# First loads on two queues, rows of the mask and a scaling moved to ScalarE, and a new order for one core's attention and soft-MoE kernel

## The chip, the cores and the metric

The kernel runs on one core of a Trainium2 chip. The metric is the device time of one execution in microseconds (us). TensorE is written PE, VectorE DVE, ScalarE ACT, GpSimd POOL; SP is the engine whose queue issues nearly all DMAs. Each engine takes its own instructions in program order; semaphores make one wait for another.

## The reference

Three layers in one launch: clustered attention (a query sees only the keys whose nearest centroid is the same as its own), an MLP with the activation h cos h, and a soft mixture of experts.

```python
q_assign = np.argmax(np.einsum('bhsd,hcd->bhsc', q_n, c_n), axis=-1)
k_assign = np.argmax(np.einsum('bhsd,hcd->bhsc', k_n, c_n), axis=-1)
mask = q_assign[:, :, :, None] == k_assign[:, :, None, :]
scores = scale * np.matmul(q, k.transpose(0, 1, 3, 2))
scores = np.where(mask, scores, -1000000000.0)
scores = scores - np.max(scores, axis=-1, keepdims=True)
attn = np.exp(scores)
attn = attn / (np.sum(attn, axis=-1, keepdims=True) + 1e-09)
return np.matmul(attn, v).astype(np.float32)
...
h = x @ w_in
g = h * np.cos(h)
return (g @ w_out).astype(np.float32)
...
logits = x @ phi
```

q, k and v have 4 batches of 8 heads of 768 rows of 64, in float32; there are 16 centroids a head. The MLP goes from 512 to 2048 and back for 3072 tokens; 8 experts of 4 slots follow.

## The kernel before

**Tiling.** Two heads make a pair, and there are 16 pairs, four to a batch. A pair has 12 units: two halves of the queries (384 columns) by six tiles of 128 keys. A unit `u` of pair `i` is two scores (one a head), each a matmul on line L444 and one on L445 into a PSUM tile `s` (three buffers), an `Exp` on ACT (L448), and later the product with v, `av`, four matmuls on L457. The weights of a query are summed over the keys by POOL (`psum_add`, L472 and L475, 128x768 each), for the last half of the last pair by DVE. The maximum over the keys, which must be known before the scores, has its own 24 matmuls a pair (`smax`, L398, output `sm`), each reduced by DVE (L400).

**The mask.** It is a set of extra rows in the stacked operands `st` (three stacks, one a pair in turn): `prep_mask` makes a matrix `mt` that ACT or DVE turns into rows for q (Relu) and for k (`ksc`, `kbias`). `rows0` does it for pair 0 from PSUM, `prep_rows` for the others from a copy `z` in SBUF. The maxima go into `st` as one more row (`mrow`).

**Preparing a pair.** `load` brings q and k of a pair (four DMAs of 192 KB in 256-byte pieces), `prep_T` transposes them on PE (`tpq`, `tpk`), `prep_hi` and `prep_lo` split them in a high and a low part, `prep_cl`, `prep_ct`, `prep_mx`, `prep_eq`, `prep_eqt` and `prep_mask` find the cluster. Pair 0 is prepared before the loop, pair 1 within pair 0, every other pair two pairs ahead.

**Fill work.** Between the scores stand also the conversion of the MLP's weights (`conv_do`, steps 0 to 7, mostly DVE), a product `wphi` of one weight with phi, and `prep_vm2`, which brings the sums of v into `vm`; every fourth pair it divides four columns of `vm` by the number of keys (L386, on DVE). The last pair also prepares the first rows `x` of the MLP: `xload` (DMA), `xprep` (POOL, DVE on L108, POOL), `xprep2` (a DVE cast `xhi` on L117, then POOL `xlo` on L118). After it `hchunk(0)` begins the MLP, which wants `xhi` and `xlo`.

**What sets the order.** Tables of numbers. A number is a place in steps of a quarter unit from the start of a pair; `at4` files the function under it, and the loop over units calls what is filed. `FIRST` holds for pair 0, `POS` for the others, `NEXT` for the last but one, `LAST` for the last. PSUM tiles of these helpers come from a ring of three banks (`mbank`), so that a matmul into a bank waits until what was in it three allocations ago has been read. DMAs that depend on such work are put off by some places (`defer`, `tick`).

```python
def at4(g, q, f, *args):
    x = int(q // 1)
    at(g + x // 4, x % 4, f, *args, rank=q - x if q != x else 0.5)
```

Of the kernel before, what the change touches and what calls it, by code (L numbers as in the profile page):

```python
# [26 lines left out]
def clustered_attention_then_soft_moe(  # L27
# [123 lines left out]
    with ExitStack() as a:  # L151
# [416 lines left out]
        def at4(g, q, f, *args):  # L568
# [4 lines left out]
            "T": [6.373, 11.528, 1.494, 13.982, 14.486, 33.654, 30.949, 35.077],  # L573
            "c": [16.761, 29.38],
            "m": [32.906, 33.461, 33.892, 36.352],
            "rows": [42.927, 43.406, 37.843, 44.784],
            "ld": 14.074,
            "cv": [[1.034, 2.033, 8.786, 11.369, 13.907, 15.492, 16.131, 21.325], [30.929, 31.112, 31.137, 33.2, 33.606, 45.734, 46.408, 47.171]],
            "wp": [22.116, 36.334, 39.913],
            "sm": [4.987, 20.453, 9.57, 3.163, 17.161, 28.27, 22.023, 22.389, 5.639, 8.505, 21.504, 13.714, 42.518, 38.435, 45.658, 28.472, 41.372, 32.987, 32.572, 46.42, 43.803, 14.216, 37.46, 46.62],  # L580
            "fin": [1.054, 10.448, 28.944, 34.08],
            "vm": [10.58, 37.044, 16.534],
            "cl": [0.15, 37.804],
            "av": [33.638, 33.642, 33.646, 33.65, 33.654, 33.658, 49.613, 49.617, 49.621, 49.625, 49.629, 49.633],
        }
        FIRST = {
            "T": [20.328, 20.36, 20.613, 21.309, 25.447, 42.131, 21.933, 41.385],
            "c": [24.098, 31.124],
            "m": [32.853, 33.416, 36.694, 39.399],
            "rows": [46.169, 42.999, 44.916, 44.421],  # L590
            "ld": 29.277,
            "hl1": [2.694, 14.043, 0.701, 14.865],
            "p1": [5.444, 6.225, 6.961, 7.291, 12.701, 16.512],
            "rows1": [18.334, 19.702, 20.194, 19.98],
            "one1": 14.9,
            "ld2": 13.561,
            "cl0": 43.548,
            "sm0": [0.941, 3.151, 0.197, 3.54, 1.676, 0.262, 18.252, 14.507, 12.716, 14.226, 11.662, 8.624, 17.928, 5.408, 5.772, 5.77, 14.195, 18.006],
            "fin0": [5.588, 6.623, 18.81, 19.962],
            "sm1": [35.319, 25.814, 36.921, 23.206, 28.928, 37.373, 24.99, 34.359, 29.894, 38.356, 22.165, 30.723, 40.822, 43.201, 46.407, 38.77, 21.105, 46.907, 42.998, 42.069, 42.024, 24.818, 42.126, 45.022],  # L600
            "fin1": [40.634, 40.735],
            "vm": [6.38, 29.072],
            "av": [14.735, 18.286, 18.296, 19.275, 23.633, 36.525, 39.363, 39.373, 42.148, 42.158, 42.168, 50.924],
        }
        NEXT = {
            "cv": [[1.657, 1.738, 3.948, 9.735, 10.263, 10.858, 11.284, 15.589], [11.409, 14.59, 16.031, 18.485, 21.508, 22.267, 23.143, 35.241], [32.1, 33.717, 35.224, 35.299, 37.447, 38.77, 40.865, 41.098]],
            "wp": [19.585, 24.815, 35.776, 44.211, 46.403, 46.852],
            "sm": [29.045, 19.936, 13.95, 28.351, 21.244, 3.581, 22.034, 8.517, 6.277, 14.276, 29.342, 12.551, 45.512, 46.443, 1.803, 37.927, 42.134, 5.869, 46.734, 1.744, 44.999, 32.092, 41.07, 37.976],
            "fin": [0.955, 9.719, 33.766, 35.901],
            "vm": [24.952, 35.735, 24.526],  # L610
            "cl": [6.201, 25.817, 35.36],
            "av": [14.561, 14.571, 14.581, 15.57, 23.429, 24.055, 34.42, 34.54, 35.379, 42.698, 42.745, 53.227],
# [731 lines left out]
```

## Time and profile before

| | |
|---|---|
| median of three runs | 898.53 us (896.6 to 899.4) |
| the profiled execution | 897.9 us, its span 896.2 us |
| PE busy | 867.8 us, 97% of the span |
| DVE, ACT, POOL busy | 685.5, 631.3, 448.2 us |
| mean granted TensorE clock | 0.992 |

The profiled execution is 0.6 us under the median, and 1.7 us lie outside its span. Busy shares are means over stages with different limits. The attention ends at 454.2 us, where `hchunk(0)` starts; from 500 to 800 us PE is never idle.

### The profile page before, as it was taken

How to read it: one execution, taken by the hardware profiler on the slowest of the kernel's cores; microseconds unless marked ns; L12 is line 12 of the kernel's file. 1: busy time of each engine (PE TensorE's matmuls, PEld its weight loads, DVE VectorE, ACT ScalarE, POOL GpSimd, SP SyncE). 2: the span in 40 equal slices, each digit the busy share in tenths (PEclk: the TensorE clock that was granted, in tenths of full speed). 3: DMA queues.
4: the chain of work that ended last, by engine and by line, in shares of the span. 5: the costliest groups of instructions: out<-in, count | busy, mean ns of one | idle time of the engine just before them, and what ended most of it. 6: DMA issues, size and time to landing. Idle time of an engine off the chain costs nothing.

```text
span 896.2 us, 16761 instructions
## 1 busy us (share of the span) xinstructions
PE 867.8 (97%) x5971; PEld 621.9 (69%) x5971; DVE 685.5 (76%) x1405; ACT 631.3 (70%) x1294; POOL 448.2 (50%) x344
## 2 busy tenths in 40 slices
PE   7899999999999999999999999999999999999996
PEld 4567676767676776676567778777877787777443
DVE  6898998988999888998877777767776776766203
ACT  6688888988888988887645756765666666577323
POOL 3468888888788887888943222222222222210000
PEclk9999999999999999999999999999999999999998
DMA  7667666656666656644311433140101011178998
GB/s 163 142 169 185 168 171 166 173 153 178 161 169 175 172 158 172 167 142 147 113 35 47 142 133 120 31 142 24 48 25 49 24 42 30 40 265 324 373 348 296
DMA packets 127814, 129.50 MB, mean 145 GB/s; under 512 B 57850, under 2 KB 105204, under 8 KB 127732
## 3 DMA queue, kind: packets, MB, share of 16 engines
q1 hardware_dynamic: 126020, 128.02, 49.1%
q8 instruction: 47, 0.77, 0.4%
q10 hardware_dynamic: 1712, 0.43, 0.2%
q14 instruction: 35, 0.29, 0.1%
HBM read 86.18 MB, written 16.97 MB: 115 GB/s over the span
## 4 chain that ended last, share of the span: by engine, by line
PE 38%; issue 4%; DVE 3%; SPq 2%; DMA 2%; ACT 1%; POOL 1%; POOLq 0%; ACTq 0%
PE h L139 25%; PE gt L881 4%; PE lp L911 2%; PE accp L994 2%; SPq L840 2%; PE fo L1278 1%; DMA wh<-in_moe_w_dram 1%; DMA xr<-recs 1%; PE o L457 1%; PE so L1254 1%; PE lf L927 0%; DVE kk L148 0%; DVE gg L874 0%; POOL xlo L118 0%; PE lf L929 0%
## 5 line engine op out<-in xcount | busy, mean ns | idle before, releaser
L475 POOL TENSOR_TENSOR ps<-ps,a 128x768 f32<-128x768 f32 x124 | 233.8, 1885 | 60.6 <-ACT a L448 55.7
L139 PE MATMUL h<-wc,xhi 128*128 128x512 f32 x768 | 248.8, 405 | 0.0
L400 DVE TENSOR_REDUCE mc<-sm 128x1 f32<-128x384 f32 x384 | 200.2, 552 | 33.5 <-PE sm L398 29.8
L448 ACT ACTIVATE a<-s 128x384 f32<-128x384 f32 x384 | 179.5, 495 | 19.6 <-PE s L445 13.8
L139 PEld LDWEIGHTS h<-wc,xhi 128*128 128x128 f32 x768 | 137.1, 188 | 38.5 <-issue 11.7
L139 PE MATMUL h<-wc,xlo 128*128 128x512 f32 x384 | 152.9, 398 | 0.1
L444 PE MATMUL s<-st 96*128 96x384 f32 (+1 forms) x384 | 142.9, 372 | 1.2
L457 PE MATMUL o<-a,vt 128*64 128x384 f32 x768 | 136.1, 497 | 0.0
L445 PE MATMUL s<-st 128*128 128x384 f32 x384 | 131.1, 341 | 0.0
L869 ACT ACTIVATE kk<-kk 128x512 f32<-128x512 f32 x96 | 60.6, 631 | 96.5 <-DVE kk L148 96.3
L398 PE MATMUL sm<-st 96*128 96x384 f32 x384 | 123.3, 356 | 4.8 <-DVE mc L400 3.4
L457 PEld LDWEIGHTS o<-a,vt 128*64 128x64 f32 x768 | 52.9, 138 | 64.9 <-issue 61.0
L444 PEld LDWEIGHTS s<-st 96*128 96x128 f32 (+1 forms) x384 | 73.0, 190 | 23.9 <-issue 17.5
L139 PEld LDWEIGHTS h<-wc,xlo 128*128 128x128 f32 x384 | 72.1, 188 | 17.4 <-POOL xlo L118 0.5
L106 POOL TENSOR_TENSOR xr<-xr 128x512 f32<-128x512 f32 x24 | 32.3, 1347 | 100.0 <-DMA xr<-recs 100.0
L110 POOL TENSOR_TENSOR xr<-xr 128x512 f32<-128x512 f32 x24 | 31.5, 1313 | 101.3 <-DVE xr L108 100.3
L398 PEld LDWEIGHTS sm<-st 96*128 96x128 f32 x384 | 71.9, 190 | 13.7 <-DVE mc L400 6.9
L874 DVE SCALAR_TENSOR_TENSOR gg<-kk,h 128x512 f32<-128x512 f32 x64 | 43.9, 686 | 45.4 <-ACT kk L871 42.6
L445 PEld LDWEIGHTS s<-st 128*128 128x128 f32 x384 | 72.9, 190 | 0.0
L148 DVE SCALAR_TENSOR_TENSOR kk<-kk,h 128x512 f32<-128x512 f32 x96 | 66.0, 688 | 3.3
L472 POOL TENSOR_TENSOR ps<-a,a 128x768 f32<-128x768 f32 x31 | 56.8, 1833 | 7.0 <-ACT a L448 5.4
L146 ACT ACTIVATE kk<-h 128x512 f32<-128x512 f32 x96 | 55.9, 582 | 1.1 <-PE h L139 1.0
(238 smaller groups left out, 1427.0 us busy)
## 6 DMA issues: line engine op xcount, KB each, us to landing
st<-st SPq DMA_DIRECT2D x128, 192.0 KB
w<-in_moe_w_dram SPq DMA_DIRECT2D x8, 2048.0 KB
wh<-in_moe_w_dram SPq DMA_DIRECT2D x23, 512.0 KB
w<-in_moe_w_out_dram SPq DMA_DIRECT2D x16, 512.0 KB
w<-in_moe_w_in_dram SPq DMA_DIRECT2D x16, 512.0 KB
qt<-in_q_dram SPq DMA_DIRECT2D x32, 192.0 KB
vt<-in_v_dram SPq DMA_DIRECT2D x16, 384.0 KB
xnum<-num SPq DMA_DIRECT2D x32, 192.0 KB
```

What stands on the lines that cost most here:

```text
L139: PE.matmul(h, lhsT=x[:, d, :], rhs=wc[f][:, w, d, :], start=(n == 0), stop=(n == 3 * DT - 1))
L146: ACT.activation(out=a, in_=h, func=AF.Copy, scale=1.0 / TWO_PI)
L148: DVE.scalar_tensor_tensor(out=a, in0=a, scalar=-TWO_PI, in1=h, op0=ALU.mult, op1=ALU.add)
L398: PE.matmul(m[:, 0:QW], lhsT=st[0:96, Q1 + h, qt * P:(qt + 1) * P], rhs=st[0:96, K1 + h, half * QW:(half + 1) * QW], start=True, stop=True)
L400: DVE.tensor_reduce(out=s["mc"][:, col:col + 1], in_=m[:, 0:QW], op=ALU.max, axis=AX.X)
L444: PE.matmul(x[:, 0:QW], lhsT=st[0:n, K1 + h, ks], rhs=st[0:n, Q1 + h, qs], start=True, stop=False)
L445: PE.matmul(x[:, 0:QW], lhsT=st[:, K2 + h, ks], rhs=st[:, Q2 + h, qs], start=False, stop=True)
L448: ACT.activation(out=T[i][u][:, h, :], in_=x[:, 0:QW], func=AF.Exp, scale=scale)
L457: PE.matmul(s["o"][64 * h:64 * h + 64, 0:QW], lhsT=s["v"][:, h, kt, :], rhs=t[:, h, :], start=(kt == 0), stop=(kt == KT - 1))
L472: (DVE if i == NPAIR - 1 and qc else POOL).tensor_tensor(out=ps, in0=s[u - 1], in1=t, op=ALU.add)
L475: (DVE if i == NPAIR - 1 and qc else POOL).tensor_tensor(out=ps, in0=ps, in1=t, op=ALU.add)
L869: ACT.activation(out=r, in_=r, func=AF.Sin, scale=0.5)
```

## The change

**Loads of pair 0.** Before, both heads of q went through SP's queue and both of k through ACT's; now the first head of each goes through SP's and the second through ACT's, q ahead of k in both. **Start.** The centroids' transpose (`prep_bd`) comes behind q's transposes. `mt` of pair 0 is made twice, in two PSUM banks, one that ACT reads and one that DVE reads. The second half's q rows leave ACT's queue ahead of the first maxima and stand among the first scores (`r0c`); a k row goes from ACT to DVE, a subtraction on DVE to an earlier place, a copy from DVE to POOL. **Pair 1.** Its k rows go from DVE to ACT, as for the pairs behind. **`vm`.** The scaling of the sums goes from DVE to ACT and one pair later. **Places.** All four tables have new numbers.

```diff
-        def load(i, ek=SP):
+        def load(i, e1=SP):
...
-            for nm, src, e in (("q", q, SP), ("k", k, ek)):
+            for nm, src in (("q", q), ("k", k)):
...
-                    e.dma_start(out=t[:, :, h, :], in_=src[b, 2 * p + h].rearrange("(p t) d -> p t d", p=P))
+                    (e1 if h else SP).dma_start(out=t[:, :, h, :], in_=src[b, 2 * p + h].rearrange("(p t) d -> p t d", p=P))
...
-            g = psum.tile([P, 512], F32, tag="v", name="mt0") if i == 0 else mbank(f"mt{i}")
+            if i == 0:
+                s["mt"] = {}
+                for e, tag in ((ACT, "v"), (DVE, "m3")):
+                    s["mt"][e] = psum.tile([P, 512], F32, tag=tag, name=f"mt0{tag}")
+                    PE.matmul(s["mt"][e][:, 0:QW], lhsT=cumf, rhs=s["eqT"], start=True, stop=True)
+                return
+            g = mbank(f"mt{i}")
...
-                elif i < 2:
-                    DVE.tensor_scalar(out=st[64:96, K1 + h, c], in0=z[o:o + 32], scalar1=ksc[o:o + 32, h:h + 1], scalar2=kbias[o:o + 32, h:h + 1], op0=ALU.mult, op1=ALU.add)
...
-            if i % NP == NP - 1:
-                x = vm[:, i + 1 - NP:i + 1]
-                DVE.tensor_scalar(out=x, in0=x, scalar1=1.0 / S, scalar2=None, op0=ALU.mult)
+
+        def vm_scale(b):
+            x = vm[:, NP * b:NP * b + NP]
+            ACT.activation(out=x, in_=x, func=AF.Copy, scale=1.0 / S)
...
-            "xp": [2.511, 10.955, 18.395],
...
+            "xp": [29.876, 36.304, 38.633],
...
+        for h in range(2):
+            at4(0, FIRST["r0c"][h], rows0, 1, 0, h, ACT)
...
+                at4(g + 12, pl["vm"][1], vm_scale, j // NP)
...
-        prep_bd()
...
+            if nm == "q":
+                prep_bd()
...
-        DVE.tensor_copy(st0[0:64, K1 + 1, :], kT[64:128])
+        DVE.tensor_tensor(out=tmp[:, 1, :], in0=qT, in1=tmp[:, 0, :], op=ALU.subtract)
...
-        DVE.tensor_tensor(out=tmp[:, 1, :], in0=qT, in1=tmp[:, 0, :], op=ALU.subtract)
+        POOL.tensor_copy(st0[0:64, K1 + 1, :], kT[64:128])
...
-        rows0(1, 1, 0, ACT)
+        rows0(1, 1, 0, DVE)
...
-        for h in range(2):
-            rows0(1, 0, h, ACT)
...
+        vm_scale(B - 1)
```

**What the tables make of it: three places.** In the rows below a name ends in running numbers; the first number is that of the pair or of the converted piece.

DVE at the start, from the first copies of pair 0 to its first maxima. Before:

```order
L248 COPY bd_117<-ctp_178 64x4x16
L249 COPY bd_117<-ctp_178 64x4x16
L271 COPY qT0_182<-tpq0_1_188 128x384
L271 COPY kT0_193<-tpk0_1_199 128x384
L741 CAST st0_119<-kT0_193 64x768
L742 CAST st0_119<-qT0_182 64x768
L743 CAST st0_119<-kT0_193 64x768
L324 TENSOR_REDUCE amx0_237<-ct0_227 128x24
L329 TENSOR_TENSOR eq0_239<-ct0_227,amx0_237 128x384
L753 TENSOR_TENSOR st2_121<-qT0_182,st2_121 128x768
L370 TENSOR_SCALAR st0_119<-mt0_249,ksc_148,kbias_149 32x384
```

Now:

```order
L271 COPY qT0_178<-tpq0_1_184 128x384
L248 COPY bd_117<-ctp_189 64x4x16
L249 COPY bd_117<-ctp_189 64x4x16
L271 COPY kT0_193<-tpk0_1_199 128x384
L748 CAST st0_119<-kT0_193 64x768
L749 CAST st0_119<-qT0_178 64x768
L750 TENSOR_TENSOR st2_121<-qT0_178,st2_121 128x768
L324 TENSOR_REDUCE amx0_237<-ct0_227 128x24
L329 TENSOR_TENSOR eq0_239<-ct0_227,amx0_237 128x384
L371 TENSOR_SCALAR st0_119<-mt0m3_251,ksc_148,kbias_149 32x384 x2
L402 TENSOR_REDUCE mc0_271<-sm0_0_272 128x1
```

The copy of q stands ahead of the two copies into `bd`, the subtraction (L753, now L750) ahead of the first reduction `amx`, and two k rows in place of one stand ahead of the first maximum.

DVE in pair 0, where its second half's maxima end (`sm0`, `m6_0_1`, `mrow_0_1`) and those of pair 1 (`sm1`) begin. Before:

```order
L400 TENSOR_REDUCE mc0_269<-sm0_23_480 128x1
L400 TENSOR_REDUCE mc0_269<-sm0_12_483 128x1
L405 TENSOR_REDUCE m6_0_1_492<-mc0_269 128x6
L357 TENSOR_SCALAR st1_120<-z1_465,ksc_148,kbias_149 32x384 x2
L415 TENSOR_SCALAR mrow_0_1_502<-mrow0_1_500 6x128
L357 TENSOR_SCALAR st1_120<-z1_465,ksc_148,kbias_149 32x384 x2
L400 TENSOR_REDUCE mc1_529<-sm1_16_530 128x1
```

Now:

```order
L402 TENSOR_REDUCE mc0_271<-sm0_22_506 128x1
L402 TENSOR_REDUCE mc0_271<-sm0_17_509 128x1
L407 TENSOR_REDUCE m6_0_1_514<-mc0_271 128x6
L417 TENSOR_SCALAR mrow_0_1_537<-mrow0_1_535 6x128
L402 TENSOR_REDUCE mc1_544<-sm1_11_545 128x1
L324 TENSOR_REDUCE amx2_559<-ct2_555 128x24
L402 TENSOR_REDUCE mc1_544<-sm1_3_563 128x1
```

The four k rows of pair 1 (L357) are gone from both sides of `mrow`. They stand on ACT now, four rows on L360 around four q rows on L358, ahead of the copy `cs2` for pair 2:

```order
L273 ACTIVATE qT2_461<-tpq2_0_462 128x384
L360 ACTIVATE st1_120<-z1_433,kbias_149,ksc_148 32x384 x2
L273 ACTIVATE qT2_461<-tpq2_1_487 128x384
L450 ACTIVATE a0_2_369<-s0_2_1_495 128x384
L450 ACTIVATE a0_3_382<-s0_3_1_499 128x384
L358 ACTIVATE st1_120<-z1_433,hsel_143 32x384 x4
L360 ACTIVATE st1_120<-z1_433,kbias_149,ksc_148 32x384 x2
L310 ACTIVATE cs2_528<-cl2_529 128x384
L450 ACTIVATE a0_4_405<-s0_4_1_540 128x384
L450 ACTIVATE a0_5_410<-s0_5_1_548 128x384
```

`cs2` and the Exps of unit 4 and 5 (`a0_4`, `a0_5`) are behind six rows of pair 1 in a run.

POOL in the last pair: sums of v (`vs15`), weight sums (`ps15`), the low part of a converted weight (`wc`) and the first x (`xr0`, `xlo0`). Before:

```order
L377 TENSOR_TENSOR vs15_6003<-vs15_6003,vt15_5752 128x128 x4
L472 TENSOR_TENSOR ps15_0_6033<-a15_0_5987,a15_1_6013 128x768
L106 TENSOR_TENSOR xr0_5997<-xr0_5997 128x512
L110 TENSOR_TENSOR xr0_5997<-xr0_5997 128x512
L475 TENSOR_TENSOR ps15_0_6033<-ps15_0_6033,a15_2_6041 128x768
L531 TENSOR_TENSOR wc2_95<-val_29_5990,wc2_95 128x512
L475 TENSOR_TENSOR ps15_0_6033<-ps15_0_6033,a15_3_6069 128x768
L118 TENSOR_TENSOR xlo0_6099<-xr0_5997,xhi0_6098 128x512
L475 TENSOR_TENSOR ps15_0_6033<-ps15_0_6033,a15_4_6092 128x768
L475 TENSOR_TENSOR ps15_0_6033<-ps15_0_6033,a15_5_6107 128x768
L531 TENSOR_TENSOR wc3_96<-val_31_6156,wc3_96 128x512
```

Now:

```order
L378 TENSOR_TENSOR vs15_6005<-vs15_6005,vt15_5749 128x128 x4
L474 TENSOR_TENSOR ps15_0_6022<-a15_0_5995,a15_1_6014 128x768
L477 TENSOR_TENSOR ps15_0_6022<-ps15_0_6022,a15_2_6027 128x768
L477 TENSOR_TENSOR ps15_0_6022<-ps15_0_6022,a15_3_6048 128x768
L477 TENSOR_TENSOR ps15_0_6022<-ps15_0_6022,a15_4_6080 128x768
L533 TENSOR_TENSOR wc2_95<-val_29_6003,wc2_95 128x512
L477 TENSOR_TENSOR ps15_0_6022<-ps15_0_6022,a15_5_6094 128x768
L106 TENSOR_TENSOR xr0_6132<-xr0_6132 128x512
L110 TENSOR_TENSOR xr0_6132<-xr0_6132 128x512
L118 TENSOR_TENSOR xlo0_6186<-xr0_6132,xhi0_6185 128x512
L533 TENSOR_TENSOR wc3_96<-val_31_6125,wc3_96 128x512
```

The three steps for the first x stand behind all five weight sums, where they stood among them; PE asks for `xlo0` in the third matmul after the attention in both.

## Rows read from the trace of the kernel before

**Rows 1.** Waits of PE, whole span: us in total, times, longest us.

```profile
PE sm L398 <- DVE mc L400: 3.4, 3, 1.1
...
PE tpk L268 <- DVE mrow L415: 2.5, 1, 2.5
...
PE wt L540 <- DVE val L528: 1.8, 1, 1.8
```

**Rows 2.** Stages: start:end, length, busy us (count) by engine, clock, DMA share, GB/s.

```profile
22.08:56.87 34.79, 32.30 (x183) 21.70 (x183) 30.76 (x57) 24.00 (x48) 17.09 (x10) 0.95 0.63 151
56.87:431.24 374.37, 369.61 (x2381) 260.60 (x2381) 339.26 (x657) 319.65 (x676) 309.84 (x225) 1.00 0.62 165
431.24:454.21 22.97, 21.21 (x117) 12.10 (x117) 21.41 (x32) 13.85 (x32) 19.34 (x15) 0.93 0.34 109
```

**Rows 3.** Three lines on DVE: duration ns min/median/max, first and last start.

```profile
L357 DVE TENSOR_SCALAR st<-z,ksc,kbias x4: 475/1482/1956, 33.8 to 39.0; 32x384 fp32r<-32x384 f32 x4
...
L386 DVE TENSOR_SCALAR vm<-vm x4: 1384/1454/1456, 130.5 to 444.5; 128x4 f32<-128x4 f32 x4
...
L117 DVE CAST xhi<-xr x24: 419/420/2032, 440.9 to 794.0; 128x512 fp32r<-128x512 f32 x24
```

**Rows 4.** Timeline, 33 to 38 us: start, us, engine, line, op [idle before].

```profile
33.84 3.29 DVE L357 TENSOR_SCALAR st<-z,ksc,kbias 32x384 fp32r<-32x384 f32 x2
...
35.11 3.70 POOL L475 TENSOR_TENSOR ps<-ps,a 128x768 f32<-128x768 f32 x2
...
37.16 0.28 DVE L415 TENSOR_SCALAR mrow<-mrow 6x128 fp32r<-6x128 f32 x1
...
37.49 0.55 PE L268 MATMUL tpk<-ident,kt 128*128 128x128 f32 x3 [2.47 <-DVE mrow L415]
```

**Rows 5.** Timeline, 129 to 132 us, POOL and DVE.

```profile
129.68 2.23 POOL L475 TENSOR_TENSOR ps<-ps,a 128x768 f32<-128x768 f32 x1 [1.52 <-ACT a L448]
...
130.48 1.45 DVE L386 TENSOR_SCALAR vm<-vm 128x4 f32<-128x4 f32 x1
```

**Rows 6.** Timeline, 444 to 446 us, POOL and DVE.

```profile
444.00 1.81 POOL L475 TENSOR_TENSOR ps<-ps,a 128x768 f32<-128x768 f32 x1
...
444.45 1.38 DVE L386 TENSOR_SCALAR vm<-vm 128x4 f32<-128x4 f32 x1
```

**Rows 7.** Stages after the two longest stalls: granted clock is the eighth column.

```profile
35.00:45.00 10.00, 7.53 (x39) 5.34 (x39) 7.81 (x12) 5.14 (x11) 7.29 (x5) 0.83 0.35 80
445.00:455.00 10.00, 8.43 (x45) 4.83 (x46) 9.97 (x11) 4.24 (x10) 6.95 (x4) 0.83 0.26 79
```

**Rows 8.** Timeline of the start, 6 to 22 us.

```profile
6.13 1.51 PE L268 MATMUL tpq<-ident,qt 128*128 128x128 f32 x6 [0.64 <-DMA qt<-in_q_dram]
...
7.44 1.48 PE L268 MATMUL tpk<-ident,kt 128*128 128x128 f32 x6
...
14.59 0.57 ACT L366 ACTIVATE st<-mt,hsel 32x384 fp32r<-32x384 f32 x1 [0.41 <-PE mt L343]
...
15.19 0.67 DVE L370 TENSOR_SCALAR st<-mt,ksc,kbias 32x384 fp32r<-32x384 f32 x1 [0.20 <-ACT st L366]
...
20.20 1.03 ACT L366 ACTIVATE st<-mt,hsel 32x384 fp32r<-32x384 f32 x2
...
21.26 0.48 ACT L436 ACTIVATE st<-mrow 1x384 fp32r<-1x384 f32 x1
```

**Rows 9.** ACT by line, 22 to 56.9 us: count, busy us, mean ns.

```profile
L448 ACT ACTIVATE a<-s 128x384 f32<-128x384 f32 x23 | 10.6, 488 | 1.7 <-PE s L445 1.4
...
L355 ACT ACTIVATE st<-z,hsel 32x384 fp32r<-32x384 f32 x6 | 3.3, 603 | 0.1
...
L359 ACT ACTIVATE st<-z,kbias,ksc 32x384 fp32r<-32x384 f32 x4 | 2.6, 696 | 0.3 <-DVE st L298 0.3
...
L282 ACT ACTIVATE st<-kT 128x768 fp32r<-128x768 f32 x2 | 1.7, 844 | 0.1
```

**Rows 10.** The page's costliest groups: the products with v.

```profile
L457 PE MATMUL o<-a,vt 128*64 128x384 f32 x768 | 136.1, 497 | 0.0
```

More of the change, by code (lines that the diff above doesn't have):

```diff
@@ L572, in clustered_attention_then_soft_moe @@
         POS = {
[L573 to L584, printed above, removed]
+            "T": [1.047, 2.646, 9.614, 13.637, 15.71, 36.526, 29.586, 34.054],
+            "c": [15.684, 30.674],
+            "m": [30.718, 32.697, 33.599, 36.946],
+            "rows": [45.184, 42.384, 37.56, 43.121],
+            "ld": 22.438,
+            "cv": [[1.007, 2.232, 5.993, 11.869, 13.097, 15.533, 16.106, 17.265], [29.575, 29.839, 31.511, 32.725, 34.028, 45.444, 45.563, 47.115]],
@@ L585, in clustered_attention_then_soft_moe @@
+            "wp": [18.879, 36.114, 39.2],
+            "sm": [31.98, 21.325, 5.633, 22.328, 19.673, 14.072, 26.133, 24.228, 16.298, 3.292, 17.499, 7.825, 47.613, 43.467, 1.923, 27.454, 45.096, 31.611, 41.379, 37.496, 46.659, 43.485, 17.979, 40.778],
+            "fin": [1.42, 11.957, 33.979, 35.5],
+            "vm": [2.511, 37.469, 15.04],
+            "cl": [11.655, 39.245],
+            "av": [33.167, 33.171, 33.175, 33.179, 33.183, 33.187, 49.595, 49.599, 49.603, 49.607, 49.611, 49.615],
         }
@@ L586, in clustered_attention_then_soft_moe @@
         FIRST = {
[L587 to L603, printed above, removed]
+            "T": [14.651, 16.766, 13.466, 13.598, 23.49, 34.849, 28.366, 43.043],
@@ new lines, in clustered_attention_then_soft_moe @@
+            "c": [19.292, 22.017],
+            "m": [22.831, 23.277, 24.548, 31.369],
+            "rows": [40.803, 46.847, 37.33, 46.989],
+            "ld": 32.723,
+            "hl1": [10.324, 12.318, 3.903, 10.862],
+            "p1": [0.302, 4.364, 5.937, 6.552, 10.318, 12.208],
+            "rows1": [18.287, 18.752, 18.318, 15.694],
+            "one1": 16.292,
+            "ld2": 5.596,
+            "cl0": 23.523,
+            "sm0": [3.262, 1.242, 4.343, 0.013, 0.37, 0.841, 12.293, 16.429, 16.928, 18.043, 11.194, 18.105, 16.084, 6.786, 7.363, 16.089, 18.043, 11.124],
@@ L604, in clustered_attention_then_soft_moe @@
+            "fin0": [6.018, 10.08, 18.295, 19.744],
+            "sm1": [27.891, 25.323, 34.092, 23.243, 31.711, 30.347, 36.076, 23.4, 29.515, 24.72, 32.332, 21.993, 42.896, 40.896, 41.675, 29.907, 46.768, 38.581, 45.836, 38.135, 47.943, 46.503, 47.424, 44.965],
+            "fin1": [36.34, 40.402],
+            "vm": [7.946, 27.234],
+            "av": [16.401, 18.347, 18.357, 18.367, 23.494, 24.326, 30.644, 39.72, 40.058, 46.249, 46.366, 47.508],
+            "r0c": [0.284, 1.721],
         }
@@ L609, in clustered_attention_then_soft_moe @@
[L609 to L612, printed above, removed]
+            "cv": [[2.229, 2.53, 2.742, 6.628, 7.028, 7.35, 8.086, 17.35], [12.103, 13.869, 16.629, 22.216, 24.098, 24.282, 28.277, 32.594], [31.283, 32.67, 36.18, 36.486, 37.167, 39.477, 42.393, 42.461]],
+            "wp": [26.086, 36.567, 44.261, 46.437, 47.015, 47.752],
@@ L613, in clustered_attention_then_soft_moe @@
+            "sm": [16.559, 17.679, 4.172, 16.852, 22.828, 27.631, 9.027, 3.32, 11.657, 31.753, 31.038, 13.531, 47.22, 46.887, 25.907, 43.195, 47.665, 45.282, 46.63, 38.9, 31.715, 37.518, 44.243, 20.15],
+            "fin": [1.429, 4.399, 36.054, 36.575],
+            "vm": [1.676, 42.012, 16.502],
+            "cl": [1.7, 10.886, 32.593],
+            "av": [14.165, 14.271, 14.281, 14.291, 23.234, 23.489, 34.616, 36.273, 36.431, 43.22, 43.964, 46.894],
         }
         LAST = {
-            "cv": [[1.208, 2.499, 4.952, 6.307, 8.06, 9.071, 9.875, 14.902], [10.483, 12.593, 15.128, 16.579, 20.957, 24.106, 29.466, 30.692], [33.001, 35.031, 37.972, 41.8, 42.74, 43.601, 45.804, 47.257]],
@@ L622, in clustered_attention_then_soft_moe @@
+            "wp": [36.801, 39.125, 47.587],
+            "fin": [0.84, 9.941],
+            "vm": [4.838, 22.442, 16.648],
+            "cl": [5.143, 17.793],
+            "xp": [29.876, 36.304, 38.633],
+            "av": [14.539, 14.611, 14.621, 14.631, 27.163, 27.173, 38.082, 38.261, 38.794, 46.372, 46.582, 47.011],
         }
```

14 lines of the change are left out of this document (2 added, 12 removed).

## The prediction

> **What bounds the kernel now.** I read the stages first. Between 56.87 and 431.24 us PE is busy for 369.61 of 374.37 us, while DVE has 35 us, ACT 55 and POOL 65 free [rows 2]. So work moved among those three is worth nothing by its sum there: it counts only where PE stands still for it. In the two stages around it PE is busy for 32.30 of 34.79 us (pair 0) and 21.21 of 22.97 (last pair), and there alone the granted clock is below 1: 0.95 and 0.93 [rows 2].
>
> Next the waits of PE [rows 1]. Three kinds touch the change: 3.4 us in three waits for a maximum (`sm` for `mc`, the longest 1.1), 2.5 us in one wait of `tpk` for `mrow`, 1.8 us in one wait of `wt` for `val`. The timeline says what is late in each.
>
> At 35.02 us PE stops until 37.49, for `mrow` [rows 4]. DVE stands in two k rows of pair 1 from 33.84 to 37.13, and only then does `mrow`, 0.28 us. Such a row takes between 475 and 1956 ns [rows 3]; these two took 3.29 us beside sums on POOL that ran from 35.11 to 38.81.
>
> The scaling of `vm`, four columns, has a median of 1454 ns on DVE, for 512 elements, where casts of 65,536 (L117) take 420 [rows 3]. At 130.48 it starts while POOL sums (129.68 to 131.91) and ends at 131.93 [rows 5]; at 444.45 it ends at 445.83, POOL's sum at 445.81 [rows 6]. It lasts until POOL is through, and the maximum or the `val` behind it is late. There are four scalings, three waits for a maximum and one for `val`: each scaling has its stall.
>
> The clock is 0.83 over the 10 us after either of the two longest stalls [rows 7]: 1.7 us lost in each, as by 3.4 us at 1.2 GHz instead of 2.4. It is 1.00 over all the pairs between, with three waits of 1.1 us [rows 1, 2].
>
> **Part by part, against the profiled 897.9 us.** The matrix products are the same but for one more `mt` at the start.
>
> *A, the start: −1.6.* The first transposes waited 0.64 us for q, those of k not at all [rows 8]. With q's two heads ahead of k's on separate queues I take 0.5 of that; bounds 0 (k, or the warming matmuls, become the limit) and 0.64. DVE's first k row began 0.60 us after ACT's q row from the same bank and waited for it (14.59, 15.19); with two banks they start together: 0.60, less 0.2 for the second `mt`, half of which I expect to show (bounds 0 and 0.60; I take 0.4). The second half's q rows, 1.03 us, stand directly ahead of the maxima copies (20.20 to 21.23, then L436 at 21.26) [rows 8]; they go in among the first scores. Against that a second k row of 0.67 us stands on DVE ahead of the first maximum, half of it, 0.33, hidden while PE makes that maximum. So 0.5 + 0.4 + 1.03 − 0.33 = 1.6. The subtraction that goes forward on DVE I count at nothing, since the first `ct` must first be made and copied; if it isn't covered it puts off the first reduction by some 0.8, as ACT's copy of its shape takes [rows 9]. Bounds: +0.4 (1.03 less 0.67 and 0.8) and −2.3.
>
> A rule speaks against the two queues: the Trainium skill ("DMA: Bandwidth & Descriptors", Issuing engines are not separate DMA queues) says that DMAs of all engines run on the same 16 DMA engines, and that a second issuer saves only the issuing time. By it the 0.5 would come from the order of q and k alone, and a second queue would add nothing; no row here parts the two, and with none of it the sum would be 0.5 less.
>
> *B, pair 0: −2.7.* Gone is the stall of 2.47 us and with it, I judge, the 1.7 of clock [rows 4, 7]: −4.2. What comes in its place is on ACT. It now has four k rows for pair 1, at 0.696 us each, and the two moved q rows, and as the order shows, `cs2` stands behind six rows in a run. From its first maxima copy to `cs2` it has some ten Exps at 0.488, four k rows at 0.696, four q rows at 0.603, two copies of 0.844 and a dozen small ones near 0.49 [rows 9]: 4.9 + 2.8 + 2.4 + 1.7 + 5.9 = 17.7 us. PE's work to the same place is what it had from 22.08 to the stall at 35.02, 12.9 us, and some 2.5 more (a transpose, `cl2`, two scores): 15.4. So PE should wait near 2 us at the product for pair 2's clusters. Some of the small copies can go while ACT now waits for scores (it is busy 24.00 of 34.79 us [rows 2]), so I take 1.5, between the waits of 1.1 that left the clock alone and the 1.8 that a lower clock followed [rows 1, 7], and no loss of clock. Net −4.2 + 1.5 = −2.7. Bounds: −4.2 (no wait) and 0 (a wait of 2.5 with its clock).
>
> The Trainium skill ("ScalarE: Activation LUTs", Rules for kernel authors) would have multiply, add and relu on VectorE and not on ScalarE. The rows agree only for a DVE that runs alone, 475 ns against ACT's 696; by that the four rows would cost 4 × 0.22 = 0.9 us more than before. The median of the same four is 1482 [rows 3, 9], and the sum goes by it.
>
> *C, the scaling of `vm`, three times: −3.4.* The waits for a maximum go [rows 1]. On ACT it is one more activation on four columns; its price isn't in the trace: over 0, and under the 0.48 of one row of 384 [rows 8]. ACT's free 55 us cover it, and it stands a pair later, when nothing asks for it; without cover it would cost 0.5 each. Bounds −3.4 and −1.9.
>
> *D, the last pair: −3.0.* Here the scaling held up `val`: 1.8 us [rows 1, 6] and 1.7 of clock [rows 7]. But POOL, busy 19.34 us in the stage [rows 2], now has the three steps for the first `x` behind all its weight sums, and PE asks for `xlo0` in the third product after the attention. POOL has something to do some 1.7 us after the stage begins at the latest, and 18 to 19 us of work up to `xlo0`; that puts `xlo0` 19.6 to 21 us after the stage's start. PE, without stall and lost clock, needs 22.97 − 1.8 − 1.7 and 0.7 for a unit of `av` (136.1 us for 192 units [rows 10]) that now stands ahead of `hchunk(0)` and no longer behind: 20.2. I take a new wait of 0.5. Net −3.5 + 0.5 = −3.0; bounds −3.5 (no wait) and +1 (late by 2, with clock lost, and DVE's `val` late too: DVE is busy 21.41 of 22.97 us).
>
> *E, the 14 pairs between: +1.2.* All places are new. The waits in them that the change doesn't aim at total some 374.4 − 369.6 − 3.4 = 1.4 us [rows 1, 2], so a better order gains 1.4 at most. A worse one makes each pair a little longer; I take 0.1 us a pair less what is gained, +1.2; bounds −1.0 and +4 (0.3 a pair, from DVE's maxima or ACT's copies a little late; ACT's share there is already 85%, DVE's 91%).
>
> Sum: −1.6 − 2.7 − 3.4 − 3.0 + 1.2 = −9.5: 888.4 on the profiled time. The median of the runs stands 0.6 above that execution: **889.0**.
>
> **The rivals.** (1) *ACT starves PE in pair 0.* The wait for `cs2` exceeds 2.4 us, and the clock falls again. For it: the count of 17.7 against 15.4. Against it: an engine's queue runs ahead where its inputs allow, and half of the small copies may be earlier. B becomes 0: 891.7. (2) *`xlo0` is late.* POOL ends over 1.8 us after PE is through, and the clock falls: D becomes 0 or +0.5: 892. For it: POOL's 19.34 us with five sums in front; against it: the sums can begin as soon as the Exps are there. (3) *The change doesn't do what it says.* The scaling and the k rows were only the last thing before PE's waits; with them gone DVE is as late, by reductions or copies that POOL holds up in the same way. C and D stay and B gains nothing: 889.0 + 6.4 + 2.7 = 898, or 895 if a third of it is gained after all. Against it: each long instruction ends within 0.02 us of POOL's [rows 5, 6], and a reduction from PSUM stood right behind it. (4) *Slower: the maxima's new places.* A maximum needs a bank of the ring of three, and DVE has to empty it. With DVE at 91% of the stage [rows 2], places that bunch maxima with copies make PE wait in every one of the 14 pairs. The gains of 9.5 us are gone at 0.7 us a pair above my 0.1; at 1 us a pair the time is 889 + 14 × 0.9 = 902. For it: three waits of that very kind, of up to 1.1 us [rows 1]. Against it: matmuls and reductions are as many as before, and PE waited for hardly anything in the other 11 pairs.
>
> **The numbers.** Forecast 0.62, (1) 0.14, (2) 0.11, (3) 0.08, (4) 0.05. Within the forecast the terms' bounds, which don't all fall together, make 884.5 to 892.5; (1) and (2) lie inside or at the edge of that, and with part of (3) the range is 884.5 to 895.5, with about 0.15 left out. A difference under 0.3%, 2.7 us, can't be told from none: faster means below 895.8. All of the forecast, (1) and (2) lie there and a little of (3); 0.88. Same: the rest of (3) and a weak form of (4), 0.07. Slower: 0.05.
>
> **What would show it.** Right: no wait of `sm` for `mc` near 1.1 us and no wait of `tpk` for `mrow`; a clock near 1.00 in both stages of [rows 7]; the first scores about 1.6 us earlier; one wait of `ct2` for ACT's `cs2` of 1 to 2 us; one short wait of `h` for POOL's `xlo`; the stage between pairs 1 and 14 shorter by about 2 us. Wrong: stalls of PE in the middle pairs for `mc` or ACT's copies that add up to more than 4 us; a clock of 0.8 near 35 or 450 us; a start no earlier; or any DVE operation between SBUF tiles that is still stretched to a sum's end with PE waiting behind it.

## The result and the profile after

The changed kernel takes **889.05 us** (887.25 to 889.08) against 898.65 before: a ratio of 0.9892, 95% interval 0.9871 to 0.9912, or 9.6 us less. Run again on another occasion it took 887.75 against 897.14, a ratio of 0.9900 (0.9884 to 0.9915), 9.4 us less. The forecast was 889.0 with a range of 884.5 to 895.5.

The profiled execution has a span of 887.4 us. Four waits of PE in it, to be set beside [rows 1]: the longest of the whole span, which comes after the attention, one ahead of the first score, and the only two between the first score and `hchunk(0)` (us in total, times, longest):

```profile
PE gt L887 <- DVE gg L880: 1.4, 1, 1.4
...
PE mrow L437 <- DVE m L430: 0.9, 1, 0.9
...
PE s L446 <- ACT a L450: 0.6, 3, 0.2
...
PE ct L318 <- ACT cs L310: 0.2, 1, 0.2
```

None of the three kinds of [rows 1] is left, and the wait for `cs2` (`ct` for `cs`) that was forecast at 1.5 us is 0.2. The stages, cut as in [rows 2] at the first score, at that of pair 1, that of pair 15 and at `hchunk(0)`:

```profile
20.47:52.43 31.96, 31.50 (x179) 20.51 (x179) 26.67 (x55) 28.60 (x57) 19.39 (x11) 1.00 0.66 161
52.43:425.93 373.50, 371.62 (x2381) 261.33 (x2381) 331.45 (x653) 314.83 (x677) 310.64 (x225) 1.00 0.63 164
425.93:446.21 20.28, 20.28 (x122) 11.87 (x121) 18.33 (x31) 13.82 (x32) 17.15 (x15) 1.00 0.36 112
...
35.00:45.00 10.00, 9.75 (x58) 7.12 (x58) 8.20 (x17) 7.89 (x17) 6.73 (x5) 1.00 0.54 153
445.00:455.00 10.00, 10.00 (x50) 6.48 (x47) 7.63 (x12) 3.48 (x6) 5.75 (x6) 1.00 0.25 73
```

The clock is 1.00 everywhere here, also over the two stretches of [rows 7], and PE does not stand still once in the last pair. Beside [rows 2] the first score is 1.61 us earlier, pair 0 takes 2.83 less, pairs 1 to 14 only 0.87 less, the last pair 2.69 less: `hchunk(0)` starts 8.0 us earlier, at 446.21 in place of 454.21. What is behind it takes 441.2 us in place of 441.9, although two units of `av` that stood there before (1.4 us by [rows 10]) now stand ahead of `hchunk(0)`: pair 0 and the last pair do one unit more each, pairs 1 to 14 as many as before.

The scaling of `vm` on ACT (line 388; duration in ns, least, median, largest):

```profile
L388 ACT ACTIVATE vm<-vm x4: 195/196/197, 151.9 to 450.0; 128x4 f32<-128x4 f32 x4
```

It takes 196 ns where it took a median of 1454 on DVE [rows 3].

In the last pair the end of POOL's work and PE's first products of the MLP (start, us, engine, line, operation) meet almost exactly:

```profile
443.11 1.29 POOL L110 TENSOR_TENSOR xr<-xr 128x512 f32<-128x512 f32 x1 [1.75 <-DVE xr L108]
444.94 1.92 POOL L118 TENSOR_TENSOR xlo<-xr,xhi 128x512 fp32r<-128x512 f32 x1 [0.54 <-DVE xhi L117]
...
446.21 0.71 PE L139 MATMUL h<-wc,xhi 128*128 128x512 f32 x2
446.91 0.50 PE L139 MATMUL h<-wc,xlo 128*128 128x512 f32 x1
```

`xlo0` is there at 446.86, and PE takes it at 446.91. With the clock back and the order as it is, there are 0.05 us to spare.

### The profile page after: what moved, and what is told of

Same layout as the page of the kernel before. It is cut to its first block, busy times and chain, and to the rows that moved or that the text cites. A ratio compares the mean times of both kernels' runs of the same rounds, so it can differ in the third digit from the quotient of the medians.

```text
span 887.4 us, 16735 instructions
## 1 busy us (share of the span) xinstructions
PE 868.3 (98%) x5972; PEld 622.4 (70%) x5972; DVE 670.9 (76%) x1397; ACT 629.7 (71%) x1301; POOL 450.6 (51%) x345
## 4 chain that ended last, share of the span: by engine, by line
PE 80%; ACT 7%; issue 4%; DMA 3%; DVE 3%; SPq 2%; POOL 1%; POOLq 0%; ACTq 0%
PE h L139 25%; PE o L459 14%; PE s L446 7%; PE sm L400 7%; PE s L447 7%; PE gt L887 4%; PE lp L917 2%; PE accp L1000 2%; SPq L846 2%; ACT a L450 2%; DMA wh<-in_moe_w_dram 2%; ACT st L358 2%; PE fo L1284 1%; PE sum L484 1%; PE cl L308 1%
## 5 line engine op out<-in xcount | busy, mean ns | idle before, releaser
L450 ACT ACTIVATE a<-s 128x384 f32<-128x384 f32 x384 | 176.7, 493 | 12.8 <-PE s L447 9.8
L139 PEld LDWEIGHTS h<-wc,xhi 128*128 128x128 f32 x768 | 137.3, 189 | 37.9 <-issue 11.1
L446 PE MATMUL s<-st 96*128 96x384 f32 (+1 forms) x384 | 139.3, 363 | 1.9 <-ACT a L450 0.6
L400 PE MATMUL sm<-st 96*128 96x384 f32 x384 | 125.2, 368 | 0.2
```

The lines of the kernel that those rows point to most:

```text
L139: PE.matmul(h, lhsT=x[:, d, :], rhs=wc[f][:, w, d, :], start=(n == 0), stop=(n == 3 * DT - 1))
L400: PE.matmul(m[:, 0:QW], lhsT=st[0:96, Q1 + h, qt * P:(qt + 1) * P], rhs=st[0:96, K1 + h, half * QW:(half + 1) * QW], start=True, stop=True)
L446: PE.matmul(x[:, 0:QW], lhsT=st[0:n, K1 + h, ks], rhs=st[0:n, Q1 + h, qs], start=True, stop=False)
L450: ACT.activation(out=T[i][u][:, h, :], in_=x[:, 0:QW], func=AF.Exp, scale=scale)
```

## The experiments

All ratios are to the kernel before on the same chip, whose median was 897.14 to 897.21 us in the three groups of runs, so that the times below can be set beside each other. The times in the expectations are counted from the 898.65 and 889.05 of the first result, which lie some 1.4 us higher than the same two kernels here (897.2 and 887.75); what is to be compared is the differences. A unit of `av` takes 0.71 us [rows 10]; where one moves from a pair to the next, both change by that.

**The scaling alone.** The kernel before with

```diff
-            if i % NP == NP - 1:
...
-                DVE.tensor_scalar(out=x, in0=x, scalar1=1.0 / S, ...)
+        def vm_scale(b):
...
+            ACT.activation(out=x, in_=x, func=AF.Copy, scale=1.0 / S)
...
+                at4(g + 12, pl["vm"][1], vm_scale, j // NP)
...
+        vm_scale(B - 1)
```

> The kernel before, with the scaling of vm alone moved to ACT and one pair later; all places as before. Theory (each scaling on DVE waited for POOL's sum, and PE waited behind it): the three waits of sm for mc go, 3.4 us, and in the last pair the stall of 1.8 us with the 1.7 us of lower clock behind it; together 6.9 us less, 891.7 us, and a clock near 1.00 from 445 to 455 us. Rival A (the places do it, the scaling was only the last thing before the wait): DVE is late by another instruction, at most 1.5 us less. Rival B (the lower clock in the last pair has nothing to do with the stall): 5.2 us less, clock still 0.83 there.

Measured: 890.24 us, ratio 0.9927 (0.9915 to 0.9939), 6.95 us less. The pairs 2 to 13 take 318.75 us in place of 321.80, the last pair 19.91 in place of 22.97, and its clock is 1.00:

```profile
35.00:45.00 10.00, 9.10 (x49) 7.30 (x49) 7.93 (x15) 5.88 (x12) 6.40 (x5) 0.83 0.42 95
445.00:455.00 10.00, 10.00 (x51) 6.52 (x51) 8.78 (x14) 3.70 (x10) 5.92 (x5) 1.00 0.16 53
```

Nearly three quarters of the change's gain is this one edit, with every place as it was. The first row shows the lower clock behind pair 0's stall still there.

**The same operation on DVE, but from PSUM.** The kernel before with

```diff
-            DVE.tensor_reduce(out=vm[:, i:i + 1], in_=g[:, 0:P], ...)
-            if i % NP == NP - 1:
...
-                DVE.tensor_scalar(out=x, in0=x, scalar1=1.0 / S, ...)
+            DVE.tensor_reduce(out=g[:, P:P + 1], in_=g[:, 0:P], ...)
+            DVE.tensor_scalar(out=vm[:, i:i + 1], in0=g[:, P:P + 1], scalar1=1.0 / S, ...)
```

> The kernel before with the scaling of vm still on DVE, but in each pair, on one column, from PSUM to SBUF (the sum of v goes to PSUM first): 16 operations in place of 4, and none of them from SBUF to SBUF. Theory (only DVE's operations between SBUF tiles wait for POOL's sums): each takes under 0.35 us, the three waits of sm for mc and the stall of the last pair go, 6.9 us less than before, the same as with the scaling on ACT. Rival (a DVE operation on so few columns is late for another reason, such as its wait for the sum ahead of it): 1 us or more each, the waits stay and there are more of them: not faster than before.

Measured: 890.55 us, ratio 0.9925 (0.9913 to 0.9938). The line's durations, and the timeline of POOL and DVE in this run at the place of [rows 5]:

```profile
L384 DVE TENSOR_SCALAR vm<-vm x16: 157/158/159, 43.5 to 439.6; 128x1 f32<-128x1 f32 x16
...
127.85 2.24 POOL L473 TENSOR_TENSOR ps<-ps,a 128x768 f32<-128x768 f32 x1 [1.52 <-ACT a L446]
...
128.66 0.16 DVE L384 TENSOR_SCALAR vm<-vm 128x1 f32<-128x1 f32 x1
```

The scaling starts and ends inside POOL's sum (127.85 to 130.09) and takes 0.16 us; 15 of the 16 lie inside such a sum. Sixteen operations on DVE that read PSUM give the same time as none (890.55 against 890.24 us); four that read and wrote SBUF cost 6.9 us. The sixteen stand where the scaling stood before, so the later place of the scaling on ACT isn't what helped either. It isn't DVE that was the wrong engine, but its SBUF to SBUF form beside POOL. The Trainium skill ("SBUF — State Buffer", Who interferes with whom) says of DVE's two-port modes, which a `tensor_scalar` can enter, that DVE and GpSimd share a pair of ports, that whoever issues first holds it for its whole instruction, and that the other blocks. The trace agrees in what can be seen: POOL's sum began first, and the scaling took a median of 1454 ns, until the sum's end [rows 5, 6], and 158 ns from PSUM; no view shows the mode itself.

**The k rows of pair 1 alone.** The kernel before without DVE's branch in `prep_rows`:

```diff
-                elif i < 2:
-                    DVE.tensor_scalar(out=st[64:96, K1 + h, c], ...)
```

> The kernel before, with the four k rows of pair 1 alone moved from DVE to ACT; all places as before. Theory: the stall of tpk for mrow (2.5 us) goes and with it the lower clock behind it (1.7 us): 4.2 us less, 894.4 us, clock near 1.00 from 35 to 45 us, less what ACT's 2.8 us of added rows make PE wait for instead (0 to 0.5 us). Rival A (ACT starves PE in pair 0 as the places of before stand): a wait of PE for an activation of 1.5 us or more takes the place, and the gain is under 1.5 us. Rival B (the lower clock has another cause than the stall): 2.5 us less, clock still 0.83.

Measured: 895.12 us, ratio 0.9981 (0.9970 to 0.9991), 2.1 less; neither the full 4.2 nor nothing. ACT and PE in pair 0:

```profile
31.79 2.61 ACT L357 ACTIVATE st<-z,kbias,ksc 32x384 fp32r<-32x384 f32 x4
34.42 1.11 ACT L355 ACTIVATE st<-z,hsel 32x384 fp32r<-32x384 f32 x2
35.55 0.87 ACT L273 ACTIVATE qT<-tpq 128x384 f32<-128x384 f32 x2
...
36.09 0.44 PE L396 MATMUL sm<-st 96*128 96x384 f32 x1 [2.00 <-ACT qT L273]
```

Six rows in a run on ACT put off the copy of `tpq`, and PE waits 2.00 us for that instead of 2.47 for `mrow`. That is the wait of rival A, though the gain is above the 1.5 us that rival A allowed, and it is the mechanism of the prediction's rival (1), with the places of before. The clock fell in this execution as before (0.83 from 35 to 45 us), and pair 0 is only 0.24 us shorter (34.55 in place of 34.79). The last pair is 1.62 us shorter (21.35 in place of 22.97), because there the lower clock stayed away behind the same stall of 1.8 us, which this edit doesn't touch. So the 2.1 us are not shown to come from pair 0.

**Both together, the places of before.** The two diffs above in one.

> The kernel before with both, the scaling of vm and the k rows of pair 1 on ACT; start and places as before. Theory (the two are independent, the new places give nothing in the middle and cost 0.2 us a pair): 6.9 + 4.2 = 11.1 us less, 887.5 us, which is 1.5 us under the changed kernel although the start is the old one. Rival (the new places carry a part of the gain of the changed kernel): at least 3 us above that, 890.5 us or more.

Measured: 890.17 us, 0.9922 (0.9909 to 0.9935): 7.0 us less in place of the theory's 11.1, no faster than the scaling alone, and on the side of the rival. The wait in pair 0:

```profile
PE sm L397 <- ACT qT L273: 2.0, 1, 2.0
```

It is that of the run before, but this time the clock stays at 1.00, and pair 0 takes 33.05 us in place of 34.69 with the scaling alone. Against that, the end of this profile, from the last product of the MLP's first layer on, takes 72.98 us in place of 71.66, and its clock fell earlier (0.76 over 870 to 880 us in place of 1.00). Whether that belongs to the kernel or to the execution, one profile of each can't tell.

**The start alone.** The kernel before with the change's lines on `load`, `prep_bd`, `mt`, `rows0` and `r0c`, the earlier subtraction and the copy on POOL:

```diff
-                    e.dma_start(out=t[:, :, h, :], ...)
+                    (e1 if h else SP).dma_start(out=t[:, :, h, :], ...)
...
+                for e, tag in ((ACT, "v"), (DVE, "m3")):
...
+            at4(0, FIRST["r0c"][h], rows0, 1, 0, h, ACT)
...
-        rows0(1, 1, 0, ACT)
+        rows0(1, 1, 0, DVE)
...
-        for h in range(2):
-            rows0(1, 0, h, ACT)
```

> The kernel before with the new start alone: loads on two queues head by head, the centroids' transpose behind q's, mt in two banks, the second half's q rows among the first scores (places 0.284 and 1.721), one k row on DVE in place of ACT, the subtraction earlier, a copy on POOL. All other places, the scaling and pair 1's k rows as before. Theory: the first score stands 1.6 us earlier, as in the changed kernel, and nothing behind it changes: 897.0 us. Rival A (the start gains only with the new places of the first pair): the first score 0.8 us earlier or less, 898 us. Rival B (the time won at the start is lost again in pair 0, where PE waits for DVE or ACT): the first score 1.6 us earlier, but the first score of pair 1 at most 0.5 us.

Measured: 897.06 us, 0.9999 (0.9990 to 1.0007): nothing, where the theory had 1.6 us less. The first score is at 19.37 us, 1.1 earlier than the 20.47 of the run with the scaling alone, which has the start of before. PE of this run, then, in a fence of its own, PE of the run with the scaling alone:

```profile
17.70 0.81 PE L438 MATMUL mrow<-ident,m 128*1 128x128 f32 x6 [0.92 <-DVE m L431]
...
21.65 0.44 PE L401 MATMUL sm<-st 96*128 96x384 f32 x1 [0.39 <-ACT st L369]
...
35.80 0.55 PE L268 MATMUL tpk<-ident,kt 128*128 128x128 f32 x3 [2.48 <-DVE mrow L418]
```

```profile
20.19 0.45 PE L399 MATMUL sm<-st 96*128 96x384 f32 x1 [0.70 <-ACT st L437]
...
35.90 0.69 PE L268 MATMUL tpk<-ident,kt 128*128 128x128 f32 x2 [2.46 <-DVE mrow L416]
```

At 35.8 us 0.1 of the 1.1 us is left, and the first score of pair 1 is no earlier (55.17 against 55.16 us): that is rival B. The same 79 products stand between the first score and the stall in both runs, and take 13.95 us in place of 12.97. Of that 0.39 is the wait for the q rows, which stood ahead of the first score and stands behind it now; the rest is busy time of PE, for which no wait is shown. The first score is a poor mark when the work around it is moved; the stall behind it is a better one.

**The changed kernel with the old start.** The lines above undone (each + of that diff out, each - in), the rest as changed.

> The changed kernel with the start of the kernel before (loads, order, one bank for mt, the q rows ahead of the maxima copies); tables, scaling and pair 1's rows as changed. Theory (the start gains about 1.1 us, which nothing swallows when the stall of pair 0 is gone): 890.2 us, the first score 1 us later, pair 0 as long. Rival (what the start wins at the first score comes back as waits among the first scores): 889.0 to 889.4 us, the first score later and pair 0 shorter by as much.

Measured: 887.99 us, 0.9899 (0.9886 to 0.9912), against 887.75 for the changed kernel: the rival's time, not the theory's 1.1 us more. Its mechanism shows only in part: the first score is 0.63 us later than in the repeated profile of the changed kernel (20.58 against 19.95), but pair 0 is only 0.1 shorter (31.85 against 31.94). So no gain of the start is measured even where no stall follows, within intervals of over 1 us to each side.

**The scaling back on DVE.** The changed kernel with the first diff of this section reversed:

```diff
-            ACT.activation(out=x, in_=x, func=AF.Copy, scale=1.0 / S)
...
+                DVE.tensor_scalar(out=x, in0=x, scalar1=1.0 / S, ...)
```

> The changed kernel with the scaling of vm back on DVE, at the place of the sums (L384). Theory (a DVE operation from SBUF to SBUF waits for POOL's sum wherever it stands, and PE soon waits for DVE): each scaling takes 1 to 1.9 us and three of four waits of sm for mc of about 1 us come back, and a stall in the last pair: 892 to 896 us. Rival (the new places leave DVE enough room): the scaling is as long, but PE waits under 0.5 us for it, 889 to 890 us.

Measured: 891.01 us, 0.9928 (0.9916 to 0.9940), 3.3 more than the changed kernel. The wait and the line in this run:

```profile
PE sm L399 <- DVE mc L401: 3.4, 3, 1.1
...
L387 DVE TENSOR_SCALAR vm<-vm x4: 1240/1448/1451, 125.3 to 437.5; 128x4 f32<-128x4 f32 x4
```

The three waits of 1.1 us are back, at other places and in the same size. The fourth scaling is nearly as long (1240 ns) and costs nothing: the last pair takes 20.29 us, as with the scaling on ACT. There the new places alone are enough.

**The k rows back on DVE.** The changed kernel with the branch of `prep_rows` put back:

```diff
+                elif i < 2:
+                    DVE.tensor_scalar(out=st[64:96, K1 + h, c], ...)
```

> The changed kernel with the four k rows of pair 1 back on DVE. Theory (the same wait for POOL's sums): the rows take 1 to 2 us each where a sum runs, mrow or a maximum of pair 0 is late, PE stalls 1.5 us or more: 891 to 893 us. Rival (the rows stand elsewhere in the new order, with nothing urgent behind them): PE waits under 0.5 us, 888.5 to 889.5 us, and the 0.25 us wait of ct for cs goes.

Measured: 887.07 us, 0.9890 (0.9877 to 0.9903): not slower. DVE and POOL in this run:

```profile
27.86 0.88 DVE L360 TENSOR_SCALAR st<-z,ksc,kbias 32x384 fp32r<-32x384 f32 x2
...
31.31 3.77 POOL L479 TENSOR_TENSOR ps<-ps,a 128x768 f32<-128x768 f32 x2
...
32.93 2.37 DVE L360 TENSOR_SCALAR st<-z,ksc,kbias 32x384 fp32r<-32x384 f32 x2
35.33 0.28 DVE L419 TENSOR_SCALAR mrow<-mrow 6x128 fp32r<-6x128 f32 x1
```

Two rows begin ahead of POOL's sums and take 0.88 us together, two take 2.37 beside sums, and `mrow` stands right behind them, as in [rows 4]. But PE has other work then and does not wait for it; its one wait in pair 0 is 0.5 us for `cs2`. In the new order the engine of these rows did not matter; the places did.

**The code with the old tables.** The changed kernel with the four tables of before (`r0c` is kept). One line of `POS` as an example:

```diff
-            "c": [15.684, 30.674],
+            "c": [16.761, 29.38],
```

> The changed kernel's code (start, scaling and pair 1's k rows on ACT) with the tables of the kernel before (and the two new places 0.284 and 1.721 for the moved q rows). Theory (the new tables give back in the middle pairs, 0.2 us each, what they win in pair 0): no wait of sm for mc, middle pairs at 26.55 us as in the run with both moves, pair 0 with that run's wait of 2.0 us for a copy on ACT, the start about 1 us earlier: 889.0 us, the same as the changed kernel. Rival A (the start's gain is swallowed by that wait): 890.2 us. Rival B (the tables are worth more than they cost): 891.5 us or more.

Measured: 889.81 us, 0.9917 (0.9905 to 0.9930), about 2 us above the changed kernel. Pairs 2 to 13 take 318.75 us in place of 321.05, pair 0 34.03 in place of 31.96, with a wait of 2.01 us for ACT's copy. The stages are those of the theory, but the time is not: the theory had the changed kernel's own time, rival A 1.2 us more, rival B some 2.5 or more. The measured 2.1 lies nearest to rival B, that the new tables are worth more than they cost. It is not in the attention: `hchunk(0)` starts at 444.64 us, in the repeated profile of the changed kernel (next) at 445.65. What is behind takes 443.7 us against 440.4, and two units of `av` are 1.4 of that.

**Only `POS` as before,** and the changed kernel again beside it. The first of these two runs has no edit; in the second the whole table `POS` is that of before, as in the line above.

> The changed kernel once more, on the same chip as the three others of this call, as their measure. Expected 887.2 to 889.1 us, which are the two ends seen so far, with the first score at 20.0 to 20.7 us, pair 0 at 32.0 us and the pairs 2 to 13 at 26.75 us each.

> The changed kernel with one table of the kernel before, POS, which orders the middle pairs. Theory (the new places cost the middle pairs 0.2 us each, 2.3 us in the stage, and win nothing there): pairs 2 to 13 at 26.55 us each, no wait of sm for mc, 2.0 to 2.3 us less than the changed kernel. Rival (FIRST and NEXT fit only the new POS): the middle pairs as short, but a new wait of PE in pair 1 or 14 takes 1 us or more of it; at most 1 us less than the changed kernel.

Measured: 887.75 us, 0.9900 (0.9884 to 0.9915), for the changed kernel, and 887.43, 0.9894 (0.9878 to 0.9909), with the old `POS`. The pairs 2 to 13 of the changed kernel, then of the one with the old `POS`:

```profile
74.44:395.48 321.04, 319.25 (x2054) 225.28 (x2054) 284.25 (x560) 275.37 (x593) 265.82 (x193) 1.00 0.64 166
```

```profile
75.27:393.95 318.68, 316.97 (x2053) 225.29 (x2053) 287.16 (x560) 278.33 (x593) 265.69 (x193) 1.00 0.64 167
```

The stage is 2.36 us shorter, as the theory had it, and nearly all of it is busy time of PE: as many products but one, 155.4 ns each in place of 154.4. No wait shows it. It is no chance of one execution: pairs 2 to 13 take 318.5 to 319.0 us in all six profiles with the old `POS` and without the scaling's waits, and 320.7 to 321.1 in all four with the new. The spans of the two profiled executions differ by 1.6 us (886.0 and 884.4), the medians by 0.3, within their intervals. The three executions with the old `POS` that were not profiled have a lower granted clock (0.992 to 0.993, against 0.996 in the profiled one and 0.994 to 0.997 with the new `POS`), which may hide a gain; that is not shown. So the 0.2 us a pair are shown for the stage and not for the whole time.

**The least of the change.** The kernel before with the scaling on ACT and `FIRST`, `NEXT` and `LAST` as new (`r0c` is in the table, but nothing uses it); of the tables one line as an example:

```diff
-                DVE.tensor_scalar(out=x, in0=x, scalar1=1.0 / S, ...)
...
+            ACT.activation(out=x, in_=x, func=AF.Copy, scale=1.0 / S)
...
-            "c": [24.098, 31.124],
+            "c": [19.292, 22.017],
```

> The least of the change that should still give all of it: the kernel before with the scaling of vm on ACT and with the new tables FIRST, NEXT and LAST; start, loads, pair 1's k rows (DVE) and POS as before. Theory (the start gives nothing behind the first scores, pair 0's stall goes by the new places and not by the engine of the rows, POS costs 2.3 us): as fast as the changed kernel with the old POS, within 0.7 us, and 2 us under the changed kernel. Rival (the start or ACT's rows are worth something after all): 1 us or more above the changed kernel with the old POS.

Measured: 887.38 us, 0.9893 (0.9878 to 0.9908): as fast as the changed kernel with the old `POS` (887.43). It is 0.4 us under the changed kernel, not the 2 us expected, and no measurement here tells those two apart. Start, rows and `POS` can all stay as they were without a loss that shows.

## Why the prediction was right, and which of its terms were not

The total came out at the forecast (−9.5 on the profiled time; −8.8 between the spans, −9.6 and −9.4 between the medians). Most of it did so by the mechanism: by the medians the scaling alone gives 6.95 us, where C and the first part of D had 6.9. The new places without `POS` give 2.8 more in the least version, near B's 2.7, though not by B's account. That the sum agrees to 0.1 us is luck. A and E, forecast at −1.6 and +1.2, nearly cancel in the sum, which hides that neither is right. And between the two traces the 1.61 us of the first score, the very size of A, have another cause.

**A, the start, −1.6: wrong.** The step that failed took waits ahead of the first score as gains of the whole. The first score does come earlier, by 1.1 us with the start alone and by 0.6 in the changed kernel, but the time behind it takes that back: the start is worth 0.1 us alone and 0.2 in the changed kernel, both inside their intervals. Whether the order of q and k or the second queue brings the first score forward is not tested. The 1.61 us between the two traces come in the main from something else: in the profiled execution of before the first products were slow (last section).

**B, pair 0, −2.7: the size right, the cause partly wrong.** Measured −2.83, with one unit of `av` more in pair 0, which the prediction did not count: without it −3.5. The stall and its lost clock are gone, 4.2. The step that failed is that ACT's rows take the stall away and then starve PE for 1.5 us, by a count of ACT's work to `cs2` of 17.7 us against PE's 15.4. The counts were near, but their beginnings are not the same moment. In the changed kernel's first profile, the copy of the first maxima and the copy `cs2` on ACT, and PE's product behind it:

```profile
18.97 0.48 ACT L438 ACTIVATE st<-mrow 1x384 fp32r<-1x384 f32 x1 [1.26 <-PE mrow L437]
...
35.67 0.49 ACT L310 ACTIVATE cs<-cl 128x384 f32<-128x384 f32 x1
...
36.21 0.55 PE L318 MATMUL ct<-ident,cs 128*128 128x128 f32 x3 [0.25 <-ACT cs L310]
```

ACT needs 17.2 us from its first maxima copy (18.97 to 36.16), PE 15.5 from the first score (20.47 to 35.96). But the copy stands 1.5 us ahead of the first score, so that 0.25 us is left of the wait. Already before it stood 0.8 ahead (21.26 and 22.08 [rows 2, 8]), which the prediction left out.

Alone, with the old places, ACT's rows do starve PE (2.0 us); with the new places PE waits 0.25 us for `cs2`, and with the rows on DVE it is as fast. The new order of pair 0 took the stall away. With the places of before, the rows' move makes pair 0 shorter by 0.24 us where the clock fell behind the new wait, and by 1.64 where it did not.

**C, −3.4, and D's first part, −3.5: right.** The scaling alone on ACT gave −6.95, and −6.6 as an operation from PSUM. Back on DVE in the changed kernel it cost +3.3. The price that the trace of before didn't show is 0.196 us, inside its bounds.

**D, the last pair, −3.0: right.** Measured −2.69, one unit of `av` included, so −3.4 without it. The wait for `xlo0`, forecast at 0.5, did not come: it is there 0.05 us before it is asked for.

**E, the pairs between, +1.2: mis-sized.** Pairs 2 to 13 cost +2.3 us with the new `POS` in the traces, 0.3 between the medians. The bound of +4 held it; the reason given, maxima and copies a little late, did not show as a wait.

The rivals (2) and (4) did not happen; (3) is refuted by the scaling alone; (1) happened only where the rows moved without the new places, as a wait of 2.0 us, behind which the clock fell once in three profiles. What is left open: which changes from one product to the next make the middle pairs 0.2 us longer, why the whole time doesn't show it, and why the 1.6 us that both moves win in pair 0 over the scaling alone are in no median. Part of the answer may lie behind `hchunk(0)`: the stretch from there to the end takes 441.7 to 443.9 us in the seven profiles with the old `LAST` and 439.4 to 441.2 in the seven with the new, more than the 1.4 us of the two units of `av`. No run parts the order from the execution's own spread there.

## What to carry to other kernels

Where an engine's small operation takes many times what its size asks for, look at what ends at the same moment on another engine, and change the operands' memory before the engine. Moving work off a late engine can put the same wait on the next one: read what is queued behind it there, and where PE has other work when it ends. And a difference between two single traces is no gain yet: a stage that both versions share should first be seen to take the same time in both.
